# Batch 0's opening rearranged: half 1's cosine transforms before the sines, weights converted in parts, and the first output product in two halves

## The chip, the cores and the metric

The kernel runs on one core of a Trainium2 chip. The metric is the device time of one execution in microseconds (us). A profiled execution has a span, from its first to its last instruction, which is a little shorter than its device time. Engines: TensorE (PE, with its weight loads PEld), VectorE (DVE), ScalarE (ACT), GpSimd (POOL), and SyncE (SP), which here only issues DMAs. Each engine works through its own instructions in order; semaphores tie them together.

## The reference

```python
def _attn_ref(x):                        # x: 8 x 3072 x 256
    X = np.fft.fft(x, axis=1)
    X = np.fft.fft(X, axis=2)
    return X.real.astype(np.float32)

def _moe_ref(x, w_a, w_b, w_out):        # 256 -> 1536 -> 256
    a = x @ w_a
    b = x @ w_b
    return (a * b @ w_out).astype(np.float32)

def reference(**kwargs):
    ...
    attn_out = _attn_ref(**attn_kwargs)
    B, S, D = attn_out.shape
    x = attn_out.reshape(B * S, D)
    return _moe_ref(x=x, **moe_kwargs)
```

The weights are handed to the kernel as 64-bit floats and are turned into float32 on the chip.

## The kernel before

**The arithmetic.** The transform along the sequence is a set of matmuls against cosine and sine tables; the transform along the width is folded into w_a and w_b, which are multiplied by a small table (`wt32`) once. Products in float32 are made of parts: a value is rounded to a high part, the rest is its low part, and a product takes three matmuls (high by high, high by low, low by high).

**Batches and units.** The main loop runs over 8 batches of 36 units. A unit is a triple (batch, strip of 512 sequence positions, 128 columns of the hidden width). For each unit `mm_e` makes the even products for a and b (six matmuls, L817), `mm_o` adds the odd ones (six, L834), `post1` and `post2` form the two products a*b and split them into `gh` and `gl`, and `mm_d` multiplies them by w_out (twelve matmuls, L916; six for each of the two signs). TensorE runs one unit ahead: `mm_e` of a unit, then `mm_d` of an earlier one, then its own `mm_o`. In batch 0, the first four units of strip 0 are "seeded": ACT writes a start value into PSUM (L803) from the columns of `w128` that belong to the unit, and copies the even product out (L822) before the odd one is added on top.

**Batch 0's opening (L647 to L998), written out by hand** in the order in which each engine is to run it. Loads: SP issues the tables, the raw rows of x (three sets of four tiles, `raw_loads`) and the weights; ACT issues the first half of w_a and w_b into `STG`. VectorE folds the raw rows (`fold(r, ops)`: set r, operations by number; 8 and 10 write the sums, 9 and 11 the differences into `F`). Six transforms in float32 follow: `p0` (cosines of half 0), `n0` (the same for the middle column), `n1` (half 1 of it), `q0` (sines of half 0), `p1` and `q1` (cosines and sines of half 1). Each has `mm`, `copy` (ACT), `sums` (VectorE), and for p and q a split into the high and low parts `PQ[:, 0..3]` (`low`, `split`).

**Weights.** `Conv` turns 64-bit words into float32: two passes on ACT ("p"), three on VectorE ("a": L478, L479, L480), and for w_out a cast (b, L481) and a low part (c, L482). `cva` and `cvb` are the two halves of the first piece of w_a and w_b, `cvo` the first piece of w_out. `wha` and `whb` (`WHalf`) multiply them by `wt32` (L557), cast the result, and send one row of it into `w128` by two small DMAs from POOL (`extra`, L569 and L574). From the main loop on, `FIRST` (before or between units) and `SLOT` (inside `post2`) say at which unit a later piece is loaded, converted and multiplied: `conv_step(k, part)`, and `WChunk`, whose products are L522.

## Time and profile before

| | |
|---|---|
| median of 3 runs | 1738.57 us (1738.52 to 1738.89) |
| the profiled execution | 1738.37 us, span 1736.6 us |
| PE | 1719.6 us busy, 99% of the span |
| DVE | 1381.6 us, 80% |
| POOL | 1120.7 us, 65% |
| ACT | 664.2 us, 38% |
| DMA | 129.63 MB, mean 75 GB/s |

Busy times are sums over the whole span, and an engine that is busy may still be waiting for its own pipeline; where the time is lost is seen in the views of single stretches. All times in them are microseconds from the start of the span.

### The profile page before, as it was taken

Reading aid. Unit: us, or ns where it says so; the run is one execution under the profiler, and the core shown is the slowest. Engines: PE = TensorE matmul, PEld = TensorE weight load, DVE = VectorE, ACT = ScalarE, POOL = GpSimd, SP = SyncE. Lnnn points to the kernel's source line nnn. Section 1 sums busy time; section 2 is a strip of 40 time slices with the busy share of each in tenths; the row PEclk is TensorE's granted clock in tenths of the full one; section 3 lists DMA queues with packets and bytes.
Section 4 is the critical chain, followed back from the end, with each engine's and each line's share of the span. In section 5 each row is a group of like instructions: output and inputs, shape, how many; then the busy total and the mean of one; then the engine's idle time right before and its main releaser. Section 6 shows DMA issues by size and latency. Waiting matters only on the chain.

```text
span 1736.6 us, 22510 instructions
## 1 busy us (share of the span) xinstructions
PE 1719.6 (99%) x7772; PEld 1417.8 (82%) x7772; DVE 1381.6 (80%) x2128; ACT 664.2 (38%) x1184; POOL 1120.7 (65%) x901
## 2 busy tenths in 40 slices
PE   8999999999999999999999999999999999999999
PEld 4678788888888888888888888888888888888788
DVE  8788988787788876887777887778778888777776
ACT  5753343333433334333343334333343333433333
POOL 1777777666676675766767667766667667644443
PEclk9999999999999999999999999999999999999999
DMA  6323343211232112410233102321123211210130
GB/s 239 120 97 51 82 152 112 83 49 47 92 89 78 40 46 104 133 37 31 68 113 109 49 11 80 103 102 49 43 86 97 69 49 46 92 52 21 8 27 25
DMA packets 179713, 129.63 MB, mean 75 GB/s; under 512 B 154366, under 2 KB 157982, under 8 KB 173710
## 3 DMA queue, kind: packets, MB, share of 16 engines
q1 hardware_dynamic: 168446, 62.09, 14.0%
q0 software_dynamic: 10608, 65.06, 11.2%
q8 instruction: 61, 1.00, 0.2%
q10 hardware_dynamic: 544, 1.05, 0.2%
q14 instruction: 54, 0.44, 0.1%
HBM read 98.84 MB, written 29.29 MB: 74 GB/s over the span
## 4 chain that ended last, share of the span: by engine, by line
PE 94%; DVE 3%; ACT 1%; DMA 1%; issue 1%; POOL 0%; SPq 0%; ACTq 0%; DVEq 0%; POOLq 0%
PE d L916 42%; PE ab L817 22%; PE ab L834 22%; PE ab L180 3%; PE d L767 2%; PE ab L192 2%; PE d L232 1%; PE ab L522 1%; DVE T L824 0%; DMA stg<-in_moe_w_b_dram 0%; DMA tab<-in_tabs_dram 0%; DVE F L479 0%; DVE T L854 0%; DVE g L840 0%; DVE F L478 0%
## 5 line engine op out<-in xcount | busy, mean ns | idle before, releaser
L874 POOL TENSOR_TENSOR gl<-g,gh 128x512 fp32r<-128x512 f32 x574 | 762.5, 1350 | 487.2 <-ACT gh L845 486.0
L916 PE MATMUL d<-gh,WO 128*128 128x512 f32 x2208 | 598.8, 389 | 0.0
L854 DVE SCALAR_TENSOR_TENSOR T<-T,ab 128x512 f32<-128x512 f32 x576 | 369.2, 682 | 286.2 <-PE ab L834 285.5
L916 PEld LDWEIGHTS d<-gh,WO 128*128 128x128 f32 x2208 | 414.7, 188 | 87.1
L817 PE MATMUL ab<-PQ,W 128*128 128x512 f32 x1728 | 445.2, 393 | 2.2 <-DVE g L840 2.1
L834 PE MATMUL ab<-PQ,W 128*128 128x512 f32 x1728 | 439.8, 390 | 2.4 <-ACT T L822 2.1
L824 DVE SCALAR_TENSOR_TENSOR T<-PN,w,ab 128x512 f32<-128x512 f32 x568 | 398.7, 743 | 30.8 <-PE ab L817 29.4
L817 PEld LDWEIGHTS ab<-PQ,W 128*128 128x128 f32 x1728 | 323.2, 188 | 73.4 <-DVE g L840 4.9
L834 PEld LDWEIGHTS ab<-PQ,W 128*128 128x128 f32 x1728 | 323.4, 188 | 70.8 <-ACT T L822 3.2
L845 ACT CAST gh<-g 128x512 fp32r<-128x512 f32 x288 | 179.2, 622 | 514.6 <-DVE g L840 497.1
L916 PE MATMUL d<-gl,WO 128*128 128x512 f32 x1104 | 348.5, 389 | 0.3 <-POOL gl L874 0.3
L857 ACT COPY bc<-ab 128x512 f32<-128x512 f32 x288 | 169.1, 587 | 451.6 <-DVE T L854 451.4
L916 PEld LDWEIGHTS d<-gl,WO 128*128 128x128 f32 x1104 | 207.0, 188 | 44.7 <-POOL gl L874 1.7
L866 DVE TENSOR_TENSOR g<-T 128x512 f32<-128x512 f32 x273 | 212.4, 778 | 0.1
L840 DVE TENSOR_TENSOR g<-ab,bc 128x512 f32<-128x512 f32 x288 | 197.5, 686 | 12.0 <-ACT bc L857 9.8
L867 ACT CAST gh<-g 128x512 fp32r<-128x512 f32 x288 | 178.7, 620 | 25.3 <-DVE g L866 23.9
L932 DVE STREAM_TRANSPOSE stg<-d 128x512 f32<-128x512 f32 x92 | 57.7, 687 | 0.0
L89 POOL TENSOR_TENSOR XH<-F,XH 128x768 fp32r<-128x768 f32 x28 | 54.9, 1970 | 0.0
L101 POOL DMA_INDIRECT RAW<-in_x_dram,rix x44 | 44.3, 1007 | 10.6 <-issue 7.5
L180 PE MATMUL ab<-tab,XH 128*128 128x384 f32 x252 | 46.3, 336 | 0.0
L180 PEld LDWEIGHTS ab<-tab,XH 128*128 128x128 f32 x252 | 44.4, 188 | 1.1
L89 POOL TENSOR_TENSOR PQ<-T,PQ 128x768 fp32r<-128x768 f32 x14 | 25.9, 1848 | 20.0 <-ACT PQ L88 20.0
(194 smaller groups left out, 944.6 us busy)
## 6 DMA issues: line engine op xcount, KB each, us to landing
tab<-in_tabs_dram POOLq DMA_DIRECT2D x21, 1200.0 KB, 5.9
tab<-in_tabs_dram POOLq DMA_DIRECT2D x21, 1152.0 KB, 5.6
RAW<-in_x_dram SPq DMA_DIRECT2D x44, 256.0 KB
out_dram<-stg SPq DMA_DIRECT2D x160, 64.0 KB
out_dram<-stg SPq DMA_DIRECT2D x58, 128.0 KB
PN<-nrow SPq DMA_DIRECT2D x14, 384.0 KB
out_dram<-stg SPq DMA_DIRECT2D x96, 32.0 KB
tab<-in_tabs_dram SPq DMA_DIRECT2D x4, 600.0 KB
```

The costliest lines, as they stand in the source:

```text
L180: nc.tensor.matmul(ps, lhs(lh, kt), tab[:, kt, rh, 0:n], start=(k == 0), stop=(k == 8))
L817: nc.tensor.matmul(ab[i], wcols(lh, 0, i, ft * P, P), PQ[:, rh, st * 512 : (st + 1) * 512], start=(k == 0 and not early), stop=(k == 2), s ...
L824: nc.vector.scalar_tensor_tensor(t[:, i, :], PN[:, st * 512 : (st + 1) * 512], w128[:, i * NFT + ft : i * NFT + ft + 1], ab[i], ALU.mult, ...
L834: nc.tensor.matmul(ab[i], wcols(lh, 1, i, ft * P, P), PQ[:, 2 + rh, st * 512 : (st + 1) * 512], start=False, stop=(k == 2), skip_group_che ...
L840: nc.vector.tensor_tensor(v["g"][:, 0, :], v["ab"][0], v["bc"], ALU.mult)
L845: nc.scalar.copy(v["gh"][:, 0, :], v["g"][:, 0, :])
L854: nc.vector.scalar_tensor_tensor(t[:, i, :], t[:, i, :], 2.0, ab[i], ALU.mult, ALU.subtract)
L857: nc.scalar.copy(bc, ab[1])
L866: (nc.gpsimd if v["early"] else nc.vector).tensor_tensor(g[:, 1, ::-1], t[:, 0, :], t[:, 1, :], ALU.mult)
L867: nc.scalar.copy(gh[:, 1, :], g[:, 1, :])
L874: eng.tensor_tensor(gl[:, s, :], g[:, s, :], f32(gh[:, s, :]), ALU.subtract)
L916: nc.tensor.matmul(cur["d"][s][h], WO[:, rh, ft, h * P : (h + 1) * P], gg[lh][:, s, :], start=(ft == first and k == 0 and not seeded), sto ...
```

## The change

The first two rows of x are loaded ahead of `wt32`; the cosine tables come in thirds, the first third ahead of the third set of raw rows; the sine tables come after w_out's first piece. The first half of w_a is converted in two parts of 256 columns. p0 and n0 run third by third in turn. After n1, p1 runs at once, then the even product of unit 0, then q0 and q1 whole. The signs are applied row by row. w_out's first piece is converted in two halves (`cvo[0]`, `cvo[1]`) and their low parts are made on POOL; RAWW's in two halves as well. The first output product makes one sign right after unit 1's odd product and the other later. For seeded units the second product a*b moves from POOL to VectorE. In the main loop the conversion of the first later piece starts a unit later and is spread over two slots.

```diff
@@ -152,6 +152,10 @@
         odd = [lambda: sums(e0, 2, ALU.subtract), lambda: diffs(e1, 3, ALU.add)]
         return even, odd
 
+    def sign_row(kind, rp):
+        f = F[:, kind, 2 * rp, :]
+        nc.scalar.activation(f, f, AF.Copy, scale=sm[:, rp % 2 : rp % 2 + 1])
+
     def sign_ops(kind):
         f = F[:, kind, 0:5:4, :]
         nc.scalar.activation(f, f, AF.Copy, scale=sm[:, 0:1])
@@ -300,7 +304,11 @@
             b, half, ps, a = self.b, self.half, self.ps, self.a
             self.t = self.home if self.home is not None else t_p.tile([P, 1024], F32, tag="T", name="T")[:, 0 : 2 * J]
             combine(self.t, a, ps, P, self.quad)
-            nc.scalar.copy(PQ[:, 0, halves(half)[0]], self.t)
+            if self.home is None:
+                self.cast()
+
+        def cast(self):
+            nc.scalar.copy(PQ[:, 0, halves(self.half)[0]], self.t)
 
         def extra(self):
             if self.half == 0:
@@ -503,7 +511,7 @@
         return [WO[:, h, 4 * q : 4 * q + 4, :].rearrange("p a (o c) -> p a c o", o=2) for h in range(2)]
 
     def by_parity(v, hl):
-        return v if len(hl.shape) == 2 else v.rearrange("p (a c o) -> p a c o", a=4, o=2)
+        return v if len(hl.shape) == 2 else v.rearrange("p (a c o) -> p a c o", a=hl.shape[1], o=2)
 
     def wcols(h, eo, i, c, n):
 
@@ -547,13 +555,13 @@
 
         def __init__(self, h, u, row):
             self.h, self.row = h, row
-            self.u = u.rearrange("p (i k c) -> p k i c", i=2, k=2)
+            self.u = u.rearrange(("p (i k c) -> p k i c", "p (k i c) -> p k i c")[h], i=2, k=2)
 
         def mm(self, ps=None, at=slice(0, 2)):
             if ps:
                 self.ps = [v.rearrange("p (i c) -> p i c", i=2) for v in ps]
-            for eo in range(2):
-                for kt in range(2):
+            for kt in range(2):
+                for eo in range(2):
                     nc.tensor.matmul(
                         self.ps[eo][:, at], wt32[:, kt, eo, :], self.u[:, kt, at], start=(kt == 0), stop=(kt == 1)
                     )
@@ -609,7 +617,7 @@
     def half_load(raw, h, eng):
         for i in range(2):
             src = (w_a, w_b)[i].bitcast(U32).rearrange("(p k) f -> p k f", k=2)
-            dst = raw[:, 512 * i : 512 * (i + 1), :].rearrange("p (a b) c -> p a (b c)", a=2)
+            dst = raw.rearrange(("p (i k b) c -> p i k (b c)", "p (k i b) c -> p i k (b c)")[h], i=2, k=2)[:, i]
             eng.dma_start(dst, src[:, :, 512 * h : 512 * (h + 1)])
 
 
@@ -619,14 +627,20 @@
     for r in range(2):
         tg, tl = (g_p.tile([P, 2, 512], F32, tag=k, name="ft").rearrange("p a (b c) -> p a b c", c=D) for k in ("gh", "gl"))
         FTs.append([tg[:, 0], tg[:, 1], tl[:, 0]])
-    cva = [Conv(STG[:, i : i + 512], (ua[:, i : i + 512], sa[:, i : i + 512]), None) for i in (0, 512)]
-    cvb = Conv(RAWW, (u_s[:, 2, :], ft_[:, 0:1024]), None)
-    cvo = Conv(STG, (u_s[:, 0, :], u_s[:, 1, :]), wo_dst(0))
+    def conv(raw, us, *cuts):
+        return [Conv(raw[:, i:j], [u[:, i:j] for u in us], None) for i, j in zip(cuts, cuts[1:])]
+
+    cva = conv(STG, (ua, sa), 0, 256, 512, 1024)
+    cvb = conv(RAWW, (u_s[:, 2, :], ft_[:, 0:1024]), 0, 512, 1024)
+    cvo = [
+        Conv(STG[:, 512 * i : 512 * (i + 1)], u, [v[:, 2 * i : 2 * i + 2] for v in wo_dst(0)])
+        for i, u in enumerate(((u_s[:, 0, 0:512], u_s[:, 1, 0:512]), (fs[:, 1024:1536], fs[:, 0:512])))
+    ]
     wha = WHalf(0, ua, u_s[0:1, 2, 0:512])
     whb = WHalf(1, u_s[:, 2, :], ft_[0:1, 1024:1536])
     p0, n0, q0 = DftP(0, 0), DftN0(0), DftQ(0, 0)
     p1, n1, q1 = DftP(0, 1), DftN0(1), DftQ(0, 1)
-    p1.home, q1.t = fs[:, 1024 : 1024 + 2 * J], fs[:, 6 * J : 8 * J]
+    p1.home, q1.t = fs[:, 4 * J : 6 * J], fs[:, 6 * J : 8 * J]
 
     def rows_zero():
 
@@ -648,24 +662,31 @@
     V.memset(zero, 0.0)
     for v in ab_tiles():
         nc.tensor.matmul(v, zero[:, 0:P], zero, start=True, stop=True)
+    nc.sync.dma_start(zr[:, 0, :], x[:, 0, :])
+    nc.gpsimd.iota(rix[:, 0:2], pattern=[[-H // 2, 2]], base=H - 3, channel_multiplier=-3)
+    nc.sync.dma_start(zr[:, 1, :], x[:, H, :])
     nc.sync.dma_start(wt32.rearrange("p k e m -> p (k e m)"), wtab32)
-    nc.gpsimd.iota(rix[:, 0:2], pattern=[[-H // 2, 2]], base=H - 3, channel_multiplier=-3)
-    nc.sync.dma_start(zr[:, 0, :], x[:, 0, :])
-    nc.sync.dma_start(zr[:, 1, :], x[:, H, :])
     nc.sync.dma_start(sm, small)
-    for r in range(3):
-        raw_loads(0, r, sraw[r])
+    tabs_at = {}
     for half in range(2):
         t = tb_p.tile([P, TB], F32, tag="tab", name="tab32")
         for q in range(3):
             v = t[:, 3 * TW * q : 3 * TW * (q + 1)] if q < 2 else room.tile([P, 3 * TW], F32, name=f"tab32_{half}")
+            tabs_at[(half, q)] = v
             tab32[(half, q)] = [v[:, TW * kt : TW * (kt + 1)] for kt in range(3)]
-            if half or q == 2:
-                nc.sync.dma_start(v, tabs32[3 * half + q])
-            elif q == 1:
-                for kt in range(3):
-                    for k in range(2):
-                        nc.sync.dma_start(tab32[(0, k)][kt], tabs32[k][:, TW * kt : TW * (kt + 1)])
+
+    def tab_pieces(half, kt):
+        for q in range(2):
+            nc.sync.dma_start(tab32[(half, q)][kt], tabs32[3 * half + q][:, TW * kt : TW * (kt + 1)])
+
+    raw_loads(0, 0, sraw[0])
+    raw_loads(0, 1, sraw[1])
+    tab_pieces(0, 0)
+    raw_loads(0, 2, sraw[2])
+    tab_pieces(0, 1)
+    tab_pieces(0, 2)
+    for kt in range(3):
+        tab_pieces(1, kt)
 
     nc.gpsimd.iota(rix[:, 2:3], pattern=[[0, 1]], base=P - 1, channel_multiplier=-1)
     V.memset(F[:, 1, :, 0:1], 0.0)
@@ -680,9 +701,12 @@
             folds[r][k]()
 
     cva[0].do("a", V)
+    cva[1].do("a", V)
     fold(0, (0, 2))
-    cva[1].do("a", V)
+    cva[2].do("a", V)
     wload(STG, wo_src(0), 4)
+    for half in range(2):
+        nc.sync.dma_start(tabs_at[(half, 2)], tabs32[3 * half + 2])
     wha.mm(ab_tiles(), slice(0, 1))
     rows_zero_mm()
     wha.mm(at=slice(1, 2))
@@ -693,20 +717,23 @@
     fold(2, (0, 1, 4, 5, 8))
     p0.mm(d_tiles(0, 2), (0,))
     n0.mm(d_tiles(1, 3), (0,))
-    for m in (p0, n0):
-        m.mm(m.ps, (1, 2))
+    for kt in (1, 2):
+        p0.mm(p0.ps, (kt,))
+        n0.mm(n0.ps, (kt,))
     fold(0, (3, 6, 7, 9))
+    sign_row(1, 0)
     wha.low()
     PQ = per.tile([P, 4, H], F32R, name="PQ")
     PN = per.tile([P, H], F32, name="PN")
     p0.copy()
     p0.sums()
-    n1.mm(d_tiles(0, 2))
-    fold(0, (11,))
-    half_load(RAWW, 1, nc.sync)
-    fold(1, (2, 3))
     n0.copy()
     n0.sums()
+    n1.mm(d_tiles(0, 2))
+    p0.low(V)
+    for r in range(3):
+        fold(r, (10,))
+    p1.mm(d_tiles(1, 3))
 
 
     def row0(st, q):
@@ -858,12 +885,22 @@
         if v["early"]:
             plus(v, high)
 
+    def lo(v, s, minus=None):
+
+        if minus:
+            minus.tensor_tensor(v["g"][:, s, ::-1], v["t"][:, 0, :], v["t"][:, 1, :], ALU.mult)
+            return
+        if s:
+            nc.scalar.copy(v["gh"][:, s, :], v["g"][:, s, :])
+        nc.gpsimd.tensor_tensor(v["gl"][:, s, :], v["g"][:, s, :], f32(v["gh"][:, s, :]), ALU.subtract)
+
     def post2(v, end=False, slot=()):
         t, g, gh, gl = v["t"], v["g"], v["gh"], v["gl"]
 
         def minus():
 
-            (nc.gpsimd if v["early"] else nc.vector).tensor_tensor(g[:, 1, ::-1], t[:, 0, :], t[:, 1, :], ALU.mult)
+            e = nc.gpsimd if v["early"] and not seeded_e(v["u"]) else nc.vector
+            e.tensor_tensor(g[:, 1, ::-1], t[:, 0, :], t[:, 1, :], ALU.mult)
             nc.scalar.copy(gh[:, 1, :], g[:, 1, :])
 
         def folds():
@@ -946,55 +983,60 @@
     v, w = begun
     seeds = {}
     seed(v["u"])
-    p0.low(V)
-    fold(1, (6, 7, 9))
+    p0.extra()
+    fold(0, (11,))
+    half_load(RAWW, 1, nc.sync)
+    fold(1, (2, 3, 6, 7, 9))
+    sign_row(1, 1)
+    n1.copy()
+    n1.sums()
+    cvo[0].do("p", V)
     fold(2, (2, 3, 6, 7, 9))
-    p0.extra()
-    cvo.do("p1", V)
-    n1.copy()
-    cvo.do("p2", V)
-    sign_ops(1)
-    for r in range(3):
-        fold(r, (10,))
-    n1.sums()
-    cvo.do("s", V)
+    p1.copy()
+    sign_row(1, 2)
     q0.room()
     v["ab"], v["t"] = mm_e(v["u"])
-    q0.mm(d_tiles(1, 3))
+    q0.mm(d_tiles(0, 2))
+    sign_row(3, 0)
+    p1.sums()
+    fold(1, (11,))
+    fold(2, (11,))
+    cvb[0].do("p", V)
+    sign_row(3, 1)
+    sign_row(3, 2)
+    q1.mm(d_tiles(1, 3))
+    cvo[0].do("a", V)
     q0.copy()
     q0.sums()
-    cvo.do("t", V)
+    cvb[0].do("a", V)
     q0.split(V)
-    cvb.do("p", V)
-    p1.mm(d_tiles(0, 2))
+    cvb[1].do("p", V)
+    cvb[1].do("a", V)
+    wload(RAWW, wa_src(1), 2)
     mm_o(v["u"], v["ab"])
-    fold(1, (11,))
-    fold(2, (11,))
-    sign_ops(3)
-    cvo.do("a2", V)
-    cvo.do("b", V)
-    p1.copy()
-    cvb.do("a", V)
-    wload(RAWW, wa_src(1), 2)
-    q1.mm(d_tiles(1, 3), parts=(0,))
     whb.mm(ab_tiles())
+    q1.copy()
+    cvo[0].do("b", V)
+    cvo[0].do("c", nc.gpsimd)
+    cvo[1].do("p", V)
     post1(v, False)
+    lo(v, 1, minus=nc.gpsimd)
     seed(w["u"])
-    p1.sums()
-    cvo.do("c", V)
+    plus_high(v)
+    lo(v, 0)
+    q1.sums()
+    cvo[1].do("a", V)
+    w["ab"], w["t"] = mm_e(w["u"])
+    mm_o(w["u"], w["ab"])
+    mm_d(v, (0,))
     whb.extra()
     whb.cast(0)
     whb.cast(1)
-    plus_high(v)
-    w["ab"], w["t"] = mm_e(w["u"])
-    q1.mm(q1.ps, parts=(1,))
-    mm_o(w["u"], w["ab"])
     whb.low()
-    q1.copy()
+    lo(v, 1)
     seed((0, 0, 2))
-    post2(v)
+    p1.cast()
     p1.low()
-    q1.sums()
     nc.sync.dma_start(q1.t[0:1, :], PN[0:1, halves(1)[0]])
 
     set_p.__exit__(None, None, None)
@@ -1215,7 +1257,8 @@
     wc = {k: WChunk(c, us[k % 2][0]) for k, c in ((0, 1), (1, 4), (3, 2), (4, 5))}
 
     FIRST = {
-        1: [(weights_later,), (conv_step, 0, "p")],
+        1: [(weights_later,)],
+        2: [(conv_step, 0, "p")],
         16: [(fold_zero,), (load_part, 0)],
         25: [(nyq.turn,), (lambda: nc.gpsimd.memset(f32(FNS), 0.0),)],
         26: [(nyq.turned,)],
@@ -1223,15 +1266,12 @@
         24: [(load_part, 2)],
     }
 
-    SLOT = {2: [(q1.split,)], 5: [(row_zero,)]}
+    SLOT = {2: [(cvo[1].do, "b", V), (cvo[1].do, "c", nc.gpsimd), (q1.split,)], 5: [(row_zero,)]}
     for k in range(6):
         if k:
             SLOT.setdefault(2 * k + 2, []).append((conv_step, k, "p"))
-        SLOT.setdefault(2 * k + 3 - (k == 0), []).append((conv_step, k, "a1"))
-        if k:
-            SLOT.setdefault(2 * k + 4, []).insert(0, (conv_step, k, "a2"))
-        else:
-            SLOT[2].append((conv_step, k, "a2"))
+        SLOT.setdefault(2 * k + 3, []).append((conv_step, k, "a1"))
+        SLOT.setdefault(2 * k + 4, []).insert(0, (conv_step, k, "a2"))
         if k in wc:
             FIRST.setdefault(2 * k + 4, []).append(wc[k])
         else:
@@ -1305,7 +1345,7 @@
                     chunk(ExDown())
 
     prev = late_post = None
-    half_done = False
+    half_done = True
     pend = list(begun)
     prev = begun[-1]
     if True:
```

## Rows read from the trace of the kernel before

**Rows 1.** The page, part 1: busy time, share of span, instructions
```profile
PE 1719.6 (99%) x7772; PEld 1417.8 (82%) x7772; DVE 1381.6 (80%) x2128; ACT 664.2 (38%) x1184; POOL 1120.7 (65%) x901
```

**Rows 2.** What TensorE waited for: line, releaser, total us, times, longest
```profile
PE ab L834 <- ACT T L822: 2.1, 1, 2.1
...
PE ab L557 <- DVE u_s L480: 1.1, 1, 1.1
```

**Rows 3.** Chain of waits, 0 to 110 us: start us, us, what
```profile
16.24 11.87 PE d L232 x36
...
62.42 1.99 PE ab L834 x6
64.41 2.56 PE ab L817 x6
...
71.14 3.44 PE ab L522 x8
...
95.29 1.36 PE ab L817 x6
```

**Rows 4.** Windows: length, busy by engine, granted clock, DMA share, GB/s
```profile
64.40:65.40 1.00, 1.00 (x4) 0.81 (x3) 0.86 (x2) 0.14 (x1) 1.00 (x2) 0.50 0.92 377
```

**Rows 5.** Timeline of VectorE, 0 to 66 us: start us, us, instruction
```profile
14.01 0.43 DVE L127 TENSOR_TENSOR F<-FT 128x256 f32<-128x256 f32 x1
...
22.54 0.55 DVE L264 TENSOR_TENSOR T<-bc,d 128x384 f32<-128x384 f32 x1
...
24.54 0.55 DVE L263 TENSOR_TENSOR PN<-bc,d 128x384 f32<-128x384 f32 x1
...
27.46 0.68 DVE L143 TENSOR_TENSOR sraw<-sraw 128x512 f32<-128x512 f32 x1
...
29.79 0.15 DVE L89 TENSOR_TENSOR EX<-bc,EX 128x1 fp32r<-128x1 f32 x1
...
38.33 0.69 DVE L478 TENSOR_SCALAR u_s<-u_s 128x1024 uint32<-128x1024 uint32 x1
...
41.55 1.28 DVE L854 SCALAR_TENSOR_TENSOR T<-T,ab 128x512 f32<-128x512 f32 x2
...
54.36 1.83 DVE L478 TENSOR_SCALAR F<-F 128x1024 uint32<-128x1024 uint32 x1
```

**Rows 6.** Timeline of SP's DMA issues, 0 to 66 us
```profile
9.84 4.78 SPq L668 DMA_DIRECT2D tab<-in_tabs_dram  x6
...
51.33 0.58 SPq L499 DMA_DIRECT2D tabw<-in_moe_w_b_dram  x1
```

**Rows 7.** Windows of two stretches, columns as in rows 4
```profile
17.00:24.00 7.00, 7.00 (x23) 4.15 (x22) 6.86 (x16) 3.98 (x12) 1.15 (x2) 1.00 1.03 416
46.99:49.50 2.51, 2.51 (x10) 1.41 (x9) 1.31 (x3) 2.51 (x7) 2.50 (x4) 1.00 0.08 1
```

**Rows 8.** Timeline of ACT, 0 to 66 us
```profile
43.66 1.30 ACT L803 ACTIVATE ab<-PN,w 128x512 f32<-128x512 f32 x2 [0.76 <-DVE g L840]
...
45.63 1.07 ACT L569 COPY FT<-ab 1x512 f32<-1x512 f32 x1
...
56.85 0.83 ACT L88 CAST PQ<-F 128x768 fp32r<-128x768 f32 x1
```

**Rows 9.** Timeline of POOL, 0 to 130 us
```profile
46.99 1.07 POOL L574 DMA_DIRECT2D w<-FT  x2 [27.39 <-ACT FT L569]
```

**Rows 10.** DMA issues, 0 to 70 us: KB each, us to landing
```profile
w<-u_s POOLq DMA_DIRECT2D x2, 1.0 KB, 4.9
w<-FT POOLq DMA_DIRECT2D x2, 1.0 KB, 1.9
```

**Rows 11.** Timeline of VectorE, 60 to 135 us
```profile
77.90 1.72 DVE L478 TENSOR_SCALAR F<-F 128x1024 uint32<-128x1024 uint32 x1
79.66 1.23 DVE L479 CUSTOM_DVE_ANT_0 F<-F 128x2048 uint16<-128x2048 uint16 x1
...
84.19 1.88 DVE L480 SCALAR_TENSOR_TENSOR F<-tabw,F 128x1024 uint32<-128x1024 uint32 x1
```

## The prediction

> **What bounds the kernel now.** I read the page first: TensorE is busy 1719.6 of 1736.6 us [rows 1], so a change that leaves its work alone can win back only its idle time and whatever it runs at half clock. The list of what TensorE waited for has two of its longer waits right in the code that the diff moves [rows 2]: 1.1 us for `u_s` before `whb`, and 2.1 us for ACT's copies before an odd product. The chain of waits places the work [rows 3]: batch 0's transforms start at 16.24, and the odd product of unit 3 starts late at 62.42. The clock row shows what that last wait costs on top: two microseconds after TensorE resumes, the granted clock is 0.50 [rows 4], that is 1.2 GHz, after 2.1 us of idleness; the six matmuls each of L834 and L817 then take 1.99 and 2.56 us, where six take 1.36 at 2.4 GHz [rows 3]: 1.8 us lost, 1.9 with what follows them. The first weight product behind that place starts at 71.14, and what comes after it is the same in both kernels. So I cost the change by one number: when does that product (conversion 0's chunk, L522) start, against 71.14? The matmuls ahead of it are the same too; only waits and clock differ.
>
> **Start: 1.4 us won.** p0's first matmul starts at 16.24, while its data F is ready at 14.44 (14.01+0.43) [rows 5]; it waits for the table. In the queue of SP the table pieces are issued from 9.84 on, behind the third raw load [rows 6]; the change puts the first two before its two 256 KB. At the 416 GB/s of this stretch [rows 7] that is 1.3 us: landing near 14.8, start near 14.85. The new order of p0 and n0 (both per third) needs the third fold only at 20.0, when it is there; raw loads landing 1 us later still come before VectorE's folds read them. Table pieces for half 1 instead of whole tables cost SP issues only, not in the path. Splitting w_a's conversion lets TensorE start its first products some 1.2 us sooner, but the chain to F does not pass there: nothing.
>
> **Transforms: 2.2 us of new waits.** p0 and n0 take 24 records at 0.33 us (11.87/36) [rows 3]: done at 22.65. n1 needs p0's PSUM, which VectorE reads until 23.09 (22.54+0.55) [rows 5]; the VectorE work before that is unchanged, so n1 starts at 23.1 after a wait of 0.45. n0's sums cannot come before 24.54, as ACT first casts PQ and then copies; the fold pieces that filled 23.1 to 24.5 are moved later, so VectorE idles 1.45 us. It idles 0.8 more where `sign_row(1,1)` now stands ahead of n1's copy on ACT. Adding the VectorE pieces in order from 24.54 (n0.sums 0.95, p0.low 0.9, three sums 1.1, one difference 0.4, fold 1's five pieces 2.33 as fold 2's from 27.46 to 29.79 [rows 5], idle 0.8, n1.sums 0.95, fold 2 2.33) gives fold 2 at 34.4. TensorE: n1 and p1 3.95 each to 31.0, the even product 1.38 to 32.4, q0's first two pairs to 33.7, then a wait of 0.7; q0 ends at 37.0, q1 at 40.95. The odd product of unit 0 needs q0.split, which stands on VectorE behind p1.sums 0.95, two differences 0.7, a 512-wide conversion 1.95 (three passes, each as one of L854's two, 1.28/2 [rows 5]), q0.sums 1.0, another conversion 1.95, and its own 0.9: 41.85, a wait of 0.65. It ends at 43.0, `whb` at 46.45; whb's own wait of 1.1 is gone, since its first half needs only `cvb[0]`. `cvb[1].a` ends at 43.8; POOL converts `cvo[0]` beside it. A 1024-wide L478 beside POOL takes 1.83 where 0.69 is the free one [rows 5]; so 0 to 1.0 us for the 512-wide three, and I take 0.3. From L854 to the seed takes 2.1 us (41.55 to 43.66 [rows 5, 8]), so the seed of unit 1 comes at 46.2 and its even product waits 0.4, to 48.25.
>
> **Unit 2's seed: the largest new wait.** ACT is given `whb.extra` behind unit 1's two copies: 48.75, +1.07 [rows 8]. Its two w128 DMAs leave POOL at 49.85 and 50.4, against 46.99 before [rows 9]. Seed (0,0,2) reads these very columns, ACT is in order, and p1.cast, the copies and the next seed stand behind it. In the trace such a DMA landed 1.9 us after issue in the second case and 4.9 in the first [rows 10]; the second met idle DMA engines (share 0.08), the first full ones (1.03) [rows 7]. Before, SP held the 2 MB of later weights until 51.33 [rows 6], because the row of PN stands ahead of them and waits for q1.sums. Now q1.sums is done by 47.2, so those loads are issued at 47.9 and 48.5, behind RAW's 1 MB issued at 44.1: the engines are full until about 53.8. The bounds are therefore 51.75 and 54.75; I take 54.2, near the loaded row, since the load ends a little earlier. TensorE, done with the halved first output product at 51.2, starts unit 2 at 54.85: 3.65 us idle, and the clock falls as at 62.42, 1.9 us.
>
> By the Trainium skill (DMA: Bandwidth & Descriptors, Anatomy of one DMA and Queues, rings and completion order) a DMA has a fixed cost of about 2 us and the engines go round between rings packet by packet, so a small transfer should not queue behind 2 MB; by that the row lands near 51.9, an estimate, and the sum would be 1739.4 where mine is 1742.3. The trace agrees on idle engines (1.9) and not on full ones (4.9).
>
> **To the odd product of unit 3.** ACT from 54.2, at the spacing of its rows (45.63 to 56.85 holds the same kinds without a gap, in 15 rows [rows 8]): seed 1.24, cast 0.75, bc 0.47, two copies 0.96, cast 0.51, seed 1.24, cast 0.51, `cvo[1].b` 0.93, q1's cast 0.75, conversion 0's two passes 2.06, bc 0.47, copy 0.48, and 0.5 waiting for the slow even product: 65.1. TensorE would be there at 64.9. Against 62.42 that is 2.7 late.
>
> **Conversion 0, one unit later.** From 65.1 TensorE needs 1.36+1.36+2.72 to 70.55. VectorE: unit 2's g at 65.3, `minus` (moved from POOL) 0.65, L478 and L479 1.72+1.23 [rows 11] (L478 is 0.69 at best and 1.83 at worst [rows 5], so 1.9 to 4.0 for the two if L479 stretches alike), L854 to g 2.1, one L824 0.7: 71.7, so unit 4's odd product waits 1.15, to 73.05. Then L824 0.65, `minus` 0.65, L480 1.88 [rows 11] (at least 1.3, twice the 0.64 of 512 columns): 74.9, and the weight product starts there, 1.85 late and 3.75 after 71.14. POOL loses three products and gains the two `cvo[*].c`, which I take as even. Later conversions keep their places.
>
> **Sum.** -1.4 - 1.1 - 2.1 + 0.45 + 0.7 + 0.65 + 0.4 + 3.65 + 1.15 + 1.85 is 4.25; the low clock is paid in both (0), and 0.5 comes off for small waits that 16.24 to 71.14 holds beside its work: 3.75, as from 71.14 to 74.9. The profiled execution took 1738.37 around its span of 1736.6, the median of the runs is 0.2 above it: 1738.57 + 3.75 = 1742.3.
>
> **Rivals.** *The w128 row is in time* (lands after 1.9): ACT's chain ends at 62.1, everything behind is 3.0 earlier: 1739.3. For it: 1 KB beside 2 MB; against it: the 4.9. *Faster:* ACT keeps up, so the late odd product and its low clock go. It decides at the seed of unit 2: TensorE without waits reaches unit 3's odd product at 59.4, so the seed must start by 49.0, before `whb.extra` itself ends by my sum. Then -1.4-1.1-2.1-1.9+2.2 = -4.3: 1734.3. *Nothing changes:* my VectorE sums are 3 to 4 us too long and gains equal waits, 1738.5. *A second fall of the clock* after the waits of 1.15 and 1.85: another 1.9, 1744.2; against it, both are shorter than the 2.1 us that brought the fall.
>
> **How the numbers follow.** Forecast 0.50 (1740.5 to 1744 with both bounds of the conversions), row in time 0.20, faster 0.12, nothing 0.12, second fall 0.06. About 0.2% (3.5 us, 1742.05) can be told from no change. The forecast lies across that bound: 0.32 above, 0.18 below. Slower: 0.32+0.02+0.06 = 0.40; same 0.18+0.18+0.12 = 0.48; faster 0.12. The range 1735.5 to 1745.0 leaves out the best faster times and the worst of the second fall.
>
> **What would show it.** Right: first L232 near 14.9; VectorE idle near 23.1 to 24.5; L574's second pair issued near 50 and seed L803 right behind its landing; a TensorE gap of over 2 us between 50 and 56; L522 of conversion 0 waiting for L480. Wrong: w128 landing within 2.5 us, or L834 of unit 3 starting before 60 without a wait.

## The result and the profile after

The changed kernel takes 1747.57 us (median of 6 runs, 1746.12 to 1754.06) against 1738.55 for the kernel before on the same chip: a ratio of 1.0059, 95% interval 1.0042 to 1.0075. The forecast was 1742.3, its range ended at 1745.0. Run again later, it took 1747.14 (5 runs, 1745.79 to 1747.76; ratio 1.0047, 1.0033 to 1.0060).

What TensorE waited for in the changed kernel (columns as in [rows 2]; L830, L844, L861, L851, L488 and L530 are the L803, L817, L834, L824, L480 and L522 of before):

```profile
PE ab L844 <- ACT ab L830: 6.0, 2, 5.3
PE ab L861 <- DVE T L851: 4.6, 3, 3.6
PE ab L530 <- DVE F L488: 2.7, 3, 1.4
...
PE d L236 <- DVE F L130: 0.8, 1, 0.8
PE d L236 <- ACT zb L715: 0.7, 1, 0.7
PE ab L861 <- DVE PQ L89: 0.6, 1, 0.6
```

Neither row of [rows 2] is left in that form: `whb` no longer waits, and the copies of L822 (now L849) cost 0.2 us. In their place stand a wait of 5.3 us for a seed and one of 3.6 us for VectorE. TensorE's timeline places them:

```profile
14.36 1.53 PE L236 MATMUL d<-tab,F 128*128 128x386 f32 x4
16.57 1.56 PE L236 MATMUL d<-tab,FN 128*128 128x386 f32 x4 [0.69 <-ACT zb L715]
...
34.49 6.72 PE L236 MATMUL d<-tab,F 128*128 128x384 f32 x20 [0.75 <-DVE F L130]
...
42.03 1.43 PE L861 MATMUL ab<-PQ,W 128*128 128x512 f32 x5 [0.59 <-DVE PQ L89]
...
47.74 1.67 PE L844 MATMUL ab<-PQ,W 128*128 128x512 f32 x6 [0.74 <-ACT ab L830]
...
57.68 2.93 PE L844 MATMUL ab<-PQ,W 128*128 128x512 f32 x6 [5.27 <-ACT ab L830]
...
68.25 1.66 PE L861 MATMUL ab<-PQ,W 128*128 128x512 f32 x6 [0.20 <-ACT T L849]
...
74.66 1.66 PE L861 MATMUL ab<-PQ,W 128*128 128x512 f32 x6 [0.68 <-DVE T L851]
77.76 3.70 PE L530 MATMUL ab<-F,wt 128*128 128x512 f32 x8 [1.44 <-DVE F L488]
...
277.40 2.93 PE L861 MATMUL ab<-PQ,W 128*128 128x512 f32 x6 [3.58 <-DVE T L851]
```

The transforms start 1.9 us earlier than in [rows 3]; the weight product of conversion 0 starts at 77.76 instead of 71.14, 6.6 us later (6.8 by the timeline of the kernel before, which has it at 70.97). The seed of unit 2 is the large step, and these rows, from the timelines of SP, POOL and ACT, show why. First SP:

```profile
47.96 0.63 SPq L1040 DMA_DIRECT2D F<-PN  x1
48.63 0.58 SPq L507 DMA_DIRECT2D tabw<-in_moe_w_b_dram  x1
49.27 0.60 SPq L507 DMA_DIRECT2D tabw<-in_moe_w_out_dram  x1
```

POOL:

```profile
51.29 1.12 POOL L582 DMA_DIRECT2D w<-FT  x2 [1.09 <-ACT FT L577]
```

ACT:

```profile
49.93 1.07 ACT L577 COPY FT<-ab 1x512 f32<-1x512 f32 x1
...
56.94 1.30 ACT L830 ACTIVATE ab<-PN,w 128x512 f32<-128x512 f32 x2 [4.52 <-DMA w<-FT]
```

The DMA issues from 0 to 70 us (compare [rows 10]):

```profile
w<-u_s POOLq DMA_DIRECT2D x2, 1.0 KB, 4.8
w<-FT POOLq DMA_DIRECT2D x2, 1.0 KB, 5.4
```

SP's queue is in order: the row of PN (L1040) used to wait for q1's sums and hold back all that stands behind it. Now q1 is done earlier, so the 2 MB of later weights leave at 48.63 instead of 51.33 [rows 6]. ACT copies the row of w128 behind unit 1's work (49.93), so its DMAs leave at 51.29 instead of 46.99 [rows 9], and landing takes 5.4 us instead of 1.9 [rows 10]; the seed (56.94) waits for that. The windows show full DMA engines there, and the granted clock at 0.50 (1.2 GHz) before TensorE has taken up work again (columns as in [rows 4]):

```profile
51.00:53.00 2.00, 1.41 (x7) 0.83 (x5) 1.54 (x3) 1.42 (x3) 1.62 (x3) 1.00 0.98 399
53.00:55.00 2.00, 0.00 (x0) 0.00 (x0) 0.94 (x2) 0.00 (x0) 0.77 (x1) 0.99 0.97 352
55.00:57.00 2.00, 0.00 (x0) 0.00 (x0) 0.00 (x0) 0.06 (x1) 0.00 (x0) 0.50 0.58 216
57.00:59.00 2.00, 1.32 (x3) 1.13 (x4) 0.00 (x0) 2.00 (x4) 0.00 (x0) 0.50 0.00 0
```

The wait at 277.40 was forecast by nothing. That profiled run (1751.04) was one of two above 1750 among the 11 runs of this kernel, both in the first series; the profile of the second series (1745.79) hasn't it. Nor does any of the 59 runs of the six kernels below that are built on the changed one and keep its table loads (e1, e2, e5, e6, e8, e11) lie more than 1.5 us above its median.

### The profile page after: what moved, and what is told of

Its sections match the earlier page's. It is cut to its first block, busy times and chain, and to the rows that moved or that the text cites. A ratio compares the mean times of both kernels' runs of the same rounds, so it can differ in the third digit from the quotient of the medians.

```text
span 1749.2 us, 22535 instructions
## 1 busy us (share of the span) xinstructions
PE 1723.1 (99%) x7772; PEld 1419.3 (81%) x7772; DVE 1383.6 (79%) x2139; ACT 664.6 (38%) x1193; POOL 1118.0 (64%) x900
## 4 chain that ended last, share of the span: by engine, by line
PE 92%; DVE 3%; DMA 2%; ACT 1%; issue 1%; POOL 0%; SPq 0%; DVEq 0%; ACTq 0%; POOLq 0%
PE d L953 41%; PE ab L844 22%; PE ab L861 21%; PE ab L184 3%; PE d L794 2%; PE ab L196 2%; PE d L236 1%; PE ab L530 1%; DVE T L851 1%; DMA PN<-nrow 0%; DMA RAW<-in_x_dram 0%; DMA RAW<-in_moe_w_a_dram 0%; DMA w<-FT 0%; DVE g L867 0%; DVE T L881 0%
## 5 line engine op out<-in xcount | busy, mean ns | idle before, releaser
L844 PE MATMUL ab<-PQ,W 128*128 128x512 f32 x1728 | 445.1, 393 | 8.2 <-ACT ab L830 6.0
L861 PE MATMUL ab<-PQ,W 128*128 128x512 f32 x1728 | 441.6, 391 | 5.4 <-DVE T L851 4.6
L851 DVE SCALAR_TENSOR_TENSOR T<-PN,w,ab 128x512 f32<-128x512 f32 x568 | 398.7, 742 | 36.4 <-PE ab L844 30.0
L844 PEld LDWEIGHTS ab<-PQ,W 128*128 128x128 f32 x1728 | 323.5, 188 | 79.5 <-ACT ab L830 7.3
L861 PEld LDWEIGHTS ab<-PQ,W 128*128 128x128 f32 x1728 | 324.0, 188 | 75.1 <-DVE T L851 6.2
L903 DVE TENSOR_TENSOR g<-T 128x512 f32<-128x512 f32 x276 | 216.1, 783 | 0.1
L969 DVE STREAM_TRANSPOSE stg<-d 128x512 f32<-128x512 f32 x92 | 57.7, 688 | 0.0
```

The costliest lines, as they stand in the source:

```text
L844: nc.tensor.matmul(ab[i], wcols(lh, 0, i, ft * P, P), PQ[:, rh, st * 512 : (st + 1) * 512], start=(k == 0 and not early), stop=(k == 2), s ...
L851: nc.vector.scalar_tensor_tensor(t[:, i, :], PN[:, st * 512 : (st + 1) * 512], w128[:, i * NFT + ft : i * NFT + ft + 1], ab[i], ALU.mult, ...
L861: nc.tensor.matmul(ab[i], wcols(lh, 1, i, ft * P, P), PQ[:, 2 + rh, st * 512 : (st + 1) * 512], start=False, stop=(k == 2), skip_group_che ...
L903: e.tensor_tensor(g[:, 1, ::-1], t[:, 0, :], t[:, 1, :], ALU.mult)
```

## The experiments

Each ratio is against the kernel before, timed on the same chip; one between 0.998 and 1.002 can't be told from no change. Line numbers shift a little between the kernels.

**Later weights held until w128's columns have landed** (e1), on the changed kernel:

```diff
+    hold = [dram.tile([P, 2], F32, name=f"hold{i}") for i in range(2)]
...
     whb.extra()
+    for i in range(2):
+        nc.sync.dma_start(hold[i], w128[:, i * NFT + 2 : i * NFT + 4])
```

> The changed kernel, but SP copies w128's new columns to DRAM (2 x 1 KB) ahead of the PN row and the 2 MB of later weights, so that these are issued only once the row has landed. Theory (the weights on the DMA engines delay the row): the row lands 1.9 to 2.5 us after its issue instead of 5.4, the gap before unit 2's even product shrinks from 5.3 to about 1.5 us, the clock stays up there, and the time falls by about 5 us, to 1742 to 1743. Rival (DMAs issued from POOL are slow here because VectorE is busy, or the row is late by its ACT copy alone): landing stays near 5 us and the time stays near 1747.5. Second rival (ACT is behind anyway): the row lands early, but TensorE waits as long at unit 3's odd product, and the time falls by less than 2 us.

Measured 1742.35 (10 runs), ratio 1.0021 (1.0012 to 1.0031), 5.2 us under the changed kernel. POOL issued the row at 52.10, and SP could read it back at 54.10, 2.0 us later (POOL, SP, then TensorE):

```profile
52.10 1.12 POOL L583 DMA_DIRECT2D w<-FT  x2 [1.11 <-ACT FT L578]
```

```profile
54.10 0.81 SPq L1035 DMA_DIRECT2D hold<-w  x2
...
55.70 0.58 SPq L508 DMA_DIRECT2D tabw<-in_moe_w_b_dram  x1
```

```profile
54.92 1.65 PE L845 MATMUL ab<-PQ,W 128*128 128x512 f32 x6 [1.67 <-ACT ab L831]
```

The wait is 1.67 instead of 5.27, the six matmuls take 1.65 instead of 2.93: no slow clock. The row is issued from POOL as in the changed kernel, behind the same work; what the edit takes away is the 2 MB, which leave only at 55.70, with the small row of PN ahead of them. So their traffic delays it, and that is the largest part of the loss.

**whb.extra sooner on ACT** (e2), weights as early as in the changed kernel:

```diff
     seed(w["u"])
+    whb.extra()
     plus_high(v)
...
     mm_d(v, (0,))
-    whb.extra()
```

> The changed kernel with whb.extra on ACT right behind unit 1's seed instead of behind its copies; the later weights are loaded as early as before this edit. Theory (order on ACT and load both count): the row's DMAs are issued near 49.2 instead of 51.3 and still take about 5 us, so unit 2's even product starts about 2 us sooner, and the time falls by 2 to 3 us. Rival (ACT's order is no matter, since the row lands when the 2 MB are through): the row lands at the same 56.8, no change.

Measured 1744.69 (6 runs), 1.0035 (1.0022 to 1.0047): 2.9 us better than the first series, 2.4 better than the second. The row was issued at 50.05 in that profile and the seed ran at 56.16, about 6 us later (POOL, then ACT):

```profile
50.05 1.12 POOL L582 DMA_DIRECT2D w<-FT  x2 [2.04 <-ACT FT L577]
```

```profile
56.16 1.30 ACT L830 ACTIVATE ab<-PN,w 128x512 f32<-128x512 f32 x2 [3.56 <-DMA w<-FT]
```

TensorE's wait is 3.19 us, 2.1 less, of which 0.8 is only a shift, to a new wait at unit 1's odd product (0.83). That places 1.3 us; no row shows where the rest of the gain comes from. Issued sooner, the row spends still longer on full engines.

**Both** (e6):

> The first two experiments together: whb.extra on ACT right behind unit 1's seed, and the later weights held until its row has landed. Theory: the row lands near 52 without load, unit 2's seed is no longer what TensorE waits for (1.67 us at most 0.3), but 0.8 us of wait appears at unit 1's odd product, because extra stands ahead of the copies; 0.5 to 1.5 us better than 1742.35. Rival (ACT's total is what sets unit 3's odd product): that wait grows by as much as the seed's wait shrinks, and the time stays at 1742.3.

Measured 1740.69 (11 runs), 1.0012 (1.0003 to 1.0022). Unit 2's seed has left TensorE's list of waits; 0.87 us stand at unit 1's odd product and 1.14 at unit 3's (1.32 in e1). The waits came as expected; the gain of 1.7 us is a little above the 0.5 to 1.5.

**VectorE's idle stretches filled** (e8), on top of both:

```diff
     p0.sums()
+    fold(0, (11,))
+    fold(1, (2, 3))
     n0.copy()
...
-    fold(0, (11,))
     half_load(RAWW, 1, nc.sync)
-    fold(1, (2, 3, 6, 7, 9))
+    fold(1, (6, 7, 9))
+    n1.copy()
     sign_row(1, 1)
-    n1.copy()
     n1.sums()
```

> The kernel with both edits (extra early, later weights held), and besides VectorE's two idle stretches filled: the difference of set 0 and the first two pieces of fold 1 stand ahead of n0's sums again, and n1's copy stands ahead of the sign of row 2 on ACT. Theory (VectorE's 1.4 and 0.9 us of idle time are what q0, the first odd product and unit 1's even product wait for: 0.75, 0.6 and 0.74): those waits fall to about 0.5 in all, and the time is 1.5 to 2 us below that of both edits alone, near 1739.5. Rival (ACT sets the end of this stretch): no change.

Measured 1738.96 (11 runs), 1.0004 (0.9995 to 1.0013): 1.7 better, and no longer told from the kernel before. The waits of q0 (0.75) and of the first odd product (0.59) are gone from the list; unit 1's even product still waits 0.74, but at 46.72. Its weight product starts at 71.06.

**Conversion 0 back in its place** (e5), on e1:

```diff
-        1: [(weights_later,)],
-        2: [(conv_step, 0, "p")],
+        1: [(weights_later,), (conv_step, 0, "p")],
...
+        SLOT.setdefault(2 * k + 3 - (k == 0), []).append((conv_step, k, "a1"))
```

> The kernel of the first experiment (later weights held until w128's columns have landed), with conversion 0 back where the kernel before has it: its ACT passes after unit 1, all three VectorE passes in unit 2. Theory (moving it a unit later costs something of its own: the waits of 0.7 us at unit 4's odd product and 1.45 us at its weight product): those two go, but VectorE's passes stand ahead of unit 2's products again and the odd product of unit 3 waits 3 us or more with a slow clock, as in the kernel before; the sum is 0 to 2 us worse than 1742.35. Rival (the later place is the loss): 2 us better, 1740.3.

Measured 1741.99 (10 runs), 1.0022 (1.0013 to 1.0032): no difference from e1. The two late waits went, 1.4 and 1.6 us came at the odd products of units 2 and 3. Neither the 3 us wait with a slow clock came nor the rival's 2 us: in this kernel the two places of the conversion can't be told apart.

**Conversion 0 a unit later, alone, in the kernel before** (e9; the reverse of that diff):

> The kernel before with only conversion 0 moved a unit later (ACT passes after unit 2, two VectorE passes in unit 3, one in unit 4). Theory: VectorE is free for unit 2's products, so the 2.05 us at unit 3's odd product and the slow clock behind it (1.9) go; waits of about 0.7 and 1.45 us come at unit 4's odd product and the weight product, as in the changed kernel; the sum is 1.5 to 2 us better than 1738.6, about 1737. Rival (the sum of the waits is only moved): within 0.5 us of 1738.6.

Measured 1737.78 (11 runs), 0.9995 (0.9985 to 1.0004). In its profile the place of before's 2.1 us [rows 2] reads:

```profile
60.27 1.65 PE L834 MATMUL ab<-PQ,W 128*128 128x512 f32 x6 [0.15 <-ACT T L822]
66.92 1.65 PE L834 MATMUL ab<-PQ,W 128*128 128x512 f32 x6 [0.79 <-DVE T L824]
69.43 3.70 PE L522 MATMUL ab<-F,wt 128*128 128x512 f32 x8 [0.86 <-DVE F L480]
```

The weight product is 1.7 us earlier than in [rows 3], as expected; the 0.9 us between the medians can't be told from nothing. The kernel before doesn't pay the slow clock in every run: in the profiles of e4, e12, e13 and e15, which leave this place alone, the wait is the same 2.05 us, but the six matmuls behind it take 1.64 to 1.67 and the granted clock reads 1.00 from 62 to 70, where [rows 4] has 0.50. In e4:

```profile
64.02 1.64 PE L834 MATMUL ab<-PQ,W 128*128 128x512 f32 x6 [2.05 <-ACT T L822]
```

The transforms start 1.3 us later there (17.51), and the weight product comes at 70.95, as in the kernel before.

**The start alone, in the kernel before** (e7: order of the loads, w_a's half in two parts, p0 and n0 by thirds):

> The kernel before with the start of the change alone: rows of x first, tables in thirds with the first ahead of the third raw rows, sine tables after w_out's piece, w_a's first half in two parts, p0 and n0 third by third. Theory of the prediction: first transform near 14.4 instead of 16.24, the time falls by 1.0 to 1.4 us, to 1737.3. Rival (VectorE's order sets the chain, so what is won at 14.4 is waited for later at n1 and q0): first transform early, time within 0.5 us of 1738.6.

Measured 1738.78 (11 runs), 1.0001 (0.9992 to 1.0010). No gain. Whether by the rival's path, this profile can't say, since its first transform starts at 16.42, not near 14.4. TensorE's timeline:

```profile
7.33 3.78 PE L557 MATMUL ab<-u,wt 128*128 128x256 f32 x8 [2.08 <-DVE u L480]
...
12.85 3.78 PE L557 MATMUL ab<-u,wt 128*128 128x256 f32 x8
16.42 1.62 PE L232 MATMUL d<-tab,F 128*128 128x386 f32 x4
```

The second group takes 3.78 us, in the first profile of the changed kernel 1.99. That it ran at the slow clock is argued from its length: the granted clock reads 1.00 from 6 to 18 us in this profile, while in e6's, where the group also takes 3.78, it reads 0.50 from 10 to 18.

**The same with w_a's half in one part** (e10):

> The kernel before with the start of the change, as run alone, but w_a's first half converted in one part as before, so that TensorE takes up work near 8.6 us and not near 7.3. Theory (taking up work sooner after 2 us of idleness puts the stretch at half clock onto the products and transforms that count: there the second group of products took 3.78 us instead of 1.99): the second group takes 1.99 again, the first transform starts near 14.9, and the time falls 1.0 to 1.4 us below 1738.6. Rival (the start's gain is lost later, whatever the clock): 1738.6.

Its profiled run is the fastest of its 11, and its start is as expected:

```profile
8.21 3.46 PE L557 MATMUL ab<-u,wt 128*128 128x256 f32 x8 [2.96 <-DVE u L480]
12.75 1.99 PE L557 MATMUL ab<-u,wt 128*128 128x256 f32 x8
14.58 1.51 PE L232 MATMUL d<-tab,F 128*128 128x386 f32 x4
```

But the median is 1739.55 (1735.85 to 1739.80), 1.0001 (0.9992 to 1.0010), and the 2.5 us of the profiled run (span 1734.1 for 1736.6) are for the most part not the start's doing. Its first transform is 1.66 us earlier than in [rows 3], its `whb` only 0.31 (the kernel before, then this one):

```profile
41.69 3.70 PE L557 MATMUL ab<-u_s,wt 128*128 128x512 f32 x8 [1.14 <-DVE u_s L480]
```

```profile
41.38 3.70 PE L557 MATMUL ab<-u_s,wt 128*128 128x512 f32 x8 [1.13 <-DVE u_s L480]
...
67.99 3.60 PE L522 MATMUL ab<-F,wt 128*128 128x512 f32 x8
```

So most of the start's gain is lost before `whb`, as e7's rival has it. The weight product is 3.0 us earlier, mostly because the wait of 2.05 us at unit 3's odd product and the slow clock behind it are missing (TensorE waits 0.56 us for POOL just ahead of it instead). In the kernel before, VectorE's L478 takes 1.83 (54.36 in [rows 5]) beside a product on POOL:

```profile
54.35 1.29 POOL L866 TENSOR_TENSOR g<-T 128x512 f32<-128x512 f32 x1
```

Here POOL's product is the long one (VectorE, then POOL):

```profile
54.03 0.68 DVE L478 TENSOR_SCALAR F<-F 128x1024 uint32<-128x1024 uint32 x1
```

```profile
54.03 1.83 POOL L876 TENSOR_TENSOR g<-T 128x512 f32<-128x512 f32 x1
```

They go the same way in e16's profile (0.68 and 1.84), which has the old start, so the edit isn't needed for it. The kernel before has such times too: 5 of its 123 runs timed beside the experiments took 1736.5 us or less. That those five went this way isn't shown.

**One part, in the mended kernel** (e11, on e8):

> The changed kernel with all mends so far (extra early, later weights held, VectorE's idle stretches filled) and w_a's first half in one part. Theory of the clock at the start: 1 to 1.5 us better than with the two parts, near 1737.6. Rival (VectorE sets that stretch, and TensorE has room there): no change, 1739.0.

Measured 1739.51 (11 runs), 1.0005 (0.9996 to 1.0014); the second group took 3.68 us after a wait of 1.89, with the granted clock at 0.50 from 14 to 16. The theory of the split falls.

**The weights early in the kernel before** (e4: PN's row behind them):

> The kernel before, with one order changed: SP issues the 2 MB of later weights ahead of PN's row, so that they no longer wait for q1.sums and are on the DMA engines while w128's columns of the second half are sent (near 47 us). Theory (load delays the row): it lands about 4.9 us after issue instead of 1.9, unit 2's seed starts near 52 instead of 49.35, and the time rises by 1 to 4 us. Rival (the small DMA goes between the large ones): landing stays below 2.5 us and the time stays at 1738.5.

Measured 1739.24 (10 runs), 1.0003 (0.9993 to 1.0012). SP issued the first megabyte at 43.62, the second only at 50.02. The row left at 48.26 onto full engines (DMA share 0.87 to 1.07 from 48 to 50), but they were nearly idle from 50.25 (0.13), and the seed ran at 50.96, 2.7 us after the issue, with a wait of 0.25. The row met under 2 us of load, in the changed kernel nearly 5 (51.29 to about 56), so this decides little.

**The changed kernel again**, and **with batch 1's tables issued later** (e3: two `load_tab` moved from `DftQ.mm` to its `post`):

> The changed kernel once more, as it is, for the spread of its runs. Theory of a second, occasional loss (the load of PN for batch 1 now and then lands late beside the tables): most runs near 1746 to 1747, a few 4 to 8 us above them; a profile without that wait has a span near 1744.5. Rival (the late load is the rule in the changed kernel): the profile shows the 3.6 us wait again, and the median is above 1747.

> The changed kernel, but the two table loads that POOL issues in batch 0's last units, next to the load of the middle column's row PN for batch 1, are issued some 6 us later. Theory of the second loss (near 277 us an odd product waits 3.6 us for VectorE, which waits for PN; its load took 8.4 us beside the tables' 1.2 MB each): the row lands in about 4 us, the wait and its slow clock go, the profiled span falls from 1749 to about 1744, the median to about 1745.5, and the runs spread less than the 8 us of the changed kernel. Rival (the store of the row to DRAM is what is slow, 3.5 us instead of 1.6): the wait stays above 2 us.

Again: 1747.14 with a profiled span of 1744.0 and no wait behind PN. e3: 1746.03 (4 runs, 1745.68 to 1747.80), 1.0043 (1.0026 to 1.0060). Where the loss comes twice in 11 runs, four runs without it show nothing. So I made it come. In the profile of 1751.04 SP issued PN's load at 264.46, behind POOL's first table load (263.37) and level with the second (264.56), and ACT got the row at 272.99; in the profile without the loss it was issued at 262.45, ahead of both (263.20 and 264.39). I moved the load back in the kernel before.

> The kernel before, with only the broadcast load of PN's row for batch 1 issued some 4 us later, behind the two small transfers of the extra column, so that the two table loads from POOL are on the DMA engines ahead of it in every run. Theory of the occasional loss: the row then lands 7 to 9 us after its issue, VectorE waits for it, TensorE waits 3 to 6 us at an odd product near 268 with a slow clock behind it, and the time rises by 4 to 8 us to 1743 to 1747. Rival (the loss in the changed kernel came from the slow store to DRAM alone): the row lands within 4 us, and the time rises by less than 2 us.

> The same late load of PN's row, with the two table loads issued still later, behind it. Theory: the row has the DMA engines to itself and lands in 3 to 4 us; the time is within 1 us of 1738.7. Rival (the late issue alone costs it): the time stays as high as with the tables ahead.

No difference in either: 1738.95 (1.0002, 0.9992 to 1.0011) and 1738.84 (0.9999, 0.9989 to 1.0008). The load came only 1.3 us later (256.10), level with the first table (256.04), and the row landed in 4.6 us. Too small a move; hence the extra copy:

```diff
-            load_nyq(1, half)
+            if half == 0:
+                nc.sync.dma_start(nhop, nrow[0][1:2, 0 : 2 * J])
+                nc.sync.dma_start(PN[:, halves(half)[0]], nhop.to_broadcast([P, 2 * J]))
...
```

> The kernel before, with the middle column's row for batch 1 copied once more within DRAM (3 KB) ahead of its broadcast load, so that the load is issued some 2 to 3 us later than in the kernel before and behind both table loads, as in the slow run of the changed kernel. Theory (tables ahead of the row): it lands 7 to 9 us after issue, an odd product near 268 waits 3 to 6 us, the time is 1743 to 1747. Rival (the tables' traffic slows it little, as the last pair showed with one table ahead): it lands in 4 to 5 us and the time rises by less than 2 us.

> The same extra copy, with both table loads issued behind the row. Theory: the row lands in about 4 us and the time is within 1.5 us of 1738.7. Rival (the copy's own time is the loss): as slow as with the tables ahead.

With the tables ahead 1744.74 (6 runs), 1.0034 (1.0022 to 1.0047); with them later 1738.90 (10 runs), 1.0004 (0.9995 to 1.0014). ACT's row and TensorE's, tables ahead:

```profile
266.63 0.83 ACT L457 COPY T<-PN 1x768 f32<-1x768 f32 x1 [7.21 <-DMA PN<-nhop]
```

```profile
271.04 1.95 PE L839 MATMUL ab<-PQ,W 128*128 128x512 f32 x6 [4.12 <-DVE T L829]
```

and with the tables later:

```profile
260.93 0.83 ACT L462 COPY T<-PN 1x768 f32<-1x768 f32 x1 [1.43 <-DMA PN<-nhop]
```

Issued at 257.57 and 257.38, the row lands 9.1 and 3.6 us later. With the tables ahead it was issued behind the first table load (256.45) and level with the second (257.64), as in the profile of 1751.04; so issued it takes 5.5 us longer, and the kernel 5.8 us (1744.74 less 1738.90).

**The start and the later conversion together** (e14, on the kernel before, w_a's half in one part):

> The two parts of the change that won time in a profile, on the kernel before: the start with w_a's first half in one part, and conversion 0 a unit later. Theory: the gains add, first transform near 14.6 and no wait of 2 us at unit 3's odd product: 1.5 to 2.5 us below the kernel before, 1736.2 to 1737.2. Rival (VectorE or the w128 row becomes the limit once TensorE is 1.5 us earlier): 1737.8, as with conversion 0 alone.

Measured 1736.65 (11 runs, 1735.98 to 1737.85), 0.9991 (0.9982 to 1.0000): 2.0 us under the kernel before by the medians and the best version here, still within 0.2%. Its profile starts the transforms at 16.78, so the gain in that run is the conversion's: from `whb` to the weight product it takes 27.5 us (42.56 to 70.08), the kernel before 29.3 (41.69 to 70.97). The faster runs of the eleven left no trace.

## Why the prediction was wrong

The mechanism was the right one and its size was not. **Start:** first transform at 14.36, forecast 14.85; n0's first third then waits 0.69 (n0's data are written by ACT, which I hadn't checked), and n1 runs from 23.1 on, as forecast. (By its own figures the forecast's 22.65 should be 22.76, and the 416 GB/s are from 17 to 24 us, 402 to 409 from 10 to 16, where the table pieces load; together that is worth about 0.1 us.) That holds for both profiles of this kernel (14.36 and 14.46). In the ten profiles of other kernels with this start (three of them with w_a's half in one part) the transforms begin at 14.58 to 16.78, so the 1.4 us are not there in every run. The 16.24 that they are counted from isn't firm either: it is the earliest of seven profiles with the old start, the others have 16.43 to 17.82. **Transforms:** waits of 0.75 and 0.59 for forecast 0.7 and 0.65; the idle VectorE rows are there (1.38 and 0.94 for 1.45 and 0.8), and e8 shows what they cost. Unit 1's even product starts at 47.74 for 46.85. The part that I took as 0.3 us is in VectorE's timeline:

```profile
42.45 0.69 DVE L487 CUSTOM_DVE_ANT_0 u_s<-u_s,FT 128x1024 uint16<-128x1024 uint16 x1
43.18 1.79 DVE L488 SCALAR_TENSOR_TENSOR u_s<-RAW,u_s 128x512 uint32<-128x512 uint32 x1
```

beside POOL's `cvo[0].c` (42.81, 1.61 us). It cost 1.1, a little above the 1.0 that I had as the upper bound. **Unit 2's seed is the step that failed, a term that was mis-sized:** the row left at 51.29 for 49.85, mostly because ACT was late by that 1.1, and the seed ran 5.65 us after it for 4.35. I had cut the loaded row's 4.9 down to 4.35 because the load would end near 53.8. It ended only near 56 (DMA share 0.97 from 53 to 55 and 0.58 from 55 to 57), and the row landed 5.4 us after its issue. The seed came at 56.94 for 54.2: 2.7 of the 2.9 us by which the weight product missed 74.9, 1.4 of them by leaving late and 1.3 by landing late. **Behind it** the sums hold, in part by luck: seed to weight product 20.8 us, forecast 20.7. But the waits are 0.20, 0.68 and 1.44 for 0.2, 1.15 and 1.85, 0.9 less in all, and TensorE's work between them takes as much longer.

The price of the slow clock, "paid in both", came from one profile as well: it is paid behind the 2.05 us wait in that profile and in e7's, and not in those of e4, e12, e13 and e15. What the kernel before loses there differs from run to run, and so does what the change can win back.

By the Trainium skill (SBUF — State Buffer, Who interferes with whom) a VectorE instruction with two SBUF inputs and a GpSimd one that reads SBUF contend for the same ports, and the one that is issued second stands still; L488's 1.79 beside POOL's 1.61 agrees. The Trainium skill's fixed cost of about 2 us for one DMA (DMA: Bandwidth & Descriptors, Anatomy of one DMA) agrees with e1 (2.0) and not with full engines (5.4).

**What I left out:** that all behind the weight product is the same in both kernels. It isn't quite: the next weight product is another 0.5 us late by the timelines (93.41 behind 77.76, against 86.12 behind 70.97), and the row of PN turns into a loss of 5.2 us in the profiled run of 1751.04; the other long run (1754.06) left no trace. e15 and e16 show that such an order costs 5.8 us. Why the load then starts late is open: the store ahead of it took 3.5 us instead of 1.6, in a stretch with idle DMA engines, and no experiment touched that.

In the profile without that loss the span is 7.4 us above the kernel before (1744.0 for 1736.6), where 3.75 was forecast; the medians are 9.0 and 8.4 apart. The 1.0 to 1.6 us between are placed by no profile; a later start, as in other kernels with this start, could give them, but no such run of this kernel was traced. Of the 9 us by the medians, holding the weights gives 5.2 (4.8 counted from the second series), ACT's order 1.7 and VectorE's order 1.7; what remains is 0.4. The start's clock is not settled either.

## What to carry to other kernels

A small DMA that a queue of work waits for should be issued ahead of large loads, or the large loads made to wait for it; freeing a queue of a stall also sets free what stood behind it. When a wait is bounded by a free and a loaded row, and the load can be timed, take the loaded row whole. A DMA race that is won by a microsecond should be costed as lost in some runs. And a wait, a slow clock or a start that is read from one profile of the kernel before may be otherwise in the next run: read several before costing what their removal gives.

## What the runs showed that I had not expected

The granted clock falls during the idle stretch itself (0.50 from 55 to 57, TensorE idle from 52.4 to 57.7). Behind shorter waits it falls in some profiles and not in others: at the start it read 0.50 from 10 to 14 in e2, behind 1.88 us without work, and 1.00 in e5, behind 2.31; at unit 3's odd product 2.05 us brought 0.50 in the kernel before and left 1.00 in e4. The same eight matmuls at the start took 1.99 us in the changed kernel and 3.78 in e6. Two instructions that start within 0.01 us of each other on VectorE and GpSimd took 1.83 and 1.29 us in the kernel before and 0.68 and 1.83 in e10; in e10, where GpSimd's is the long one, the 2.05 us wait behind them is missing. A 1 KB DMA took 2.0 us on free engines and 5.4 beside 2 MB; a 384 KB broadcast 3.6 and 9.1.
